# RetNet recurrence and a SiLU layer in split float32: remainders by VectorE alone, a fourth buffer for g, chunk 2's y read back at other places

## The chip, the cores and the metric

The kernel runs on one core of a Trainium2 chip. A core has TensorE (matrix products, into the accumulators of PSUM), VectorE, ScalarE and GpSimd (elementwise work), and SyncE, which here only issues DMAs. Each engine works through a queue of its own in order, and waits on semaphores for the others. The profile calls them PE (with PEld for its loads of weights), DVE, ACT, POOL and SP. The metric is the device time of one execution in microseconds; lower is better. The executions shown for the kernel before took 593.3, 593.84 and 3425.35 us, the last far out of line, and their median is 593.84.

## The reference

Two blocks follow each other: a recurrence over time for each head, and two dense layers with SiLU between them.

```python
# q, k, v: (4, 8, 768, 64) float32; w_in: (512, 2048), w_out: (2048, 512) float64
gamma = 1.0 - 2.0 ** (-5.0 - np.arange(H))
scale = 1.0 / np.sqrt(D)
for t in range(S):
    state = gamma[None, :, None, None] * state + einsum('bhd,bhe->bhde', k[:, :, t], v[:, :, t])
    y[:, :, t] = scale * einsum('bhd,bhde->bhe', q[:, :, t], state)
x = y.transpose(0, 2, 1, 3).reshape(B * S, H * D)      # 3072 x 512
h = x @ w_in
g = h * (1.0 / (1.0 + np.exp(-h)))
out = (g @ w_out).astype(np.float32)                   # 3072 x 512
```

## The kernel before, in words

**Chunks and units.** Time is cut into six chunks of 128 steps; with four batches that makes 24 units, numbered unit = 4 * chunk + batch. For a unit the kernel turns q and k (on TensorE for the early units, by a transposing DMA for the later ones), forms scores, masks them with the decay, carries a state, and forms y in PSUM. A "visit" of number m does the y of unit m - 2, the scores of unit m - 1 and, early on, the turning of unit m (`halves`, `visit`).

**Products in three parts.** TensorE multiplies in a reduced float32. Each operand is therefore split in three: a high part, a remainder, and a mixed part, and a product is the sum of three products (parts 0 and 1 into one accumulator, `ha` or `oa`, part 2 into another, `hb` or `ob`; an elementwise combination of the two gives the result). Slices of w_in and w_out are split by `split_steps`, x by `split_x` (ScalarE the high part, L653; VectorE the other two, L656 and L659), g by `split`. The weights arrive as 64-bit floats and are first converted with integer operations by `convert_steps` (L211 to L230).

**First layer.** A step (c, f) multiplies chunk c's x (512 tokens) by column block f of w_in: eight products into ha, four into hb (`multiply`, L754). `close_steps` then has ScalarE copy ha into a buffer of g (L777) and VectorE take hb from it (L782), and `put_g` stores g to DRAM (L796). Buffers of g are three tiles of tag `hs` in the pool `hpool`; ha and hb take turns in three banks of PSUM, so a bank has to be emptied before the second next accumulator can start.

**The order of the steps** is a list written out by hand: for chunks 0, 1 and 2 the blocks are woven together, and blocks 12 to 15 of chunks 0 and 1 and blocks 8 to 15 of chunk 2 come late: (0,12) to (0,15), (1,12) to (1,15), (2,8) to (2,15); then chunks 3, 4 and 5. `takes` names the steps after which a slice of weights is converted, `behind` the steps after which a visit or a `late_y` or `late_x` stands. A visit stands behind (1,15), one behind each of (2,9), (2,11) and (2,13).

**Chunk 2's x.** Its split form first lies in a tile of the pool `wpool` (tag `wq`), which is later needed for w_in's blocks 12 to 15. So y of chunk 2 is stored to DRAM, read back by `late_y` (L682) and split a second time by `late_x`, into the tile of `xpool` that chunk 0's x has left. Step (2,8) is the first that uses this second split. `late_y` takes its buffers by turns from tag `kt` and from tag `wl`, the tile that otherwise holds the unscaled remainder of a slice of weights.

**Second layer.** Chunk by chunk, `split` reads g back, applies SiLU and splits it; TensorE multiplies by w_out (L1270, L1294), and the results are stored.

**Queues.** TensorE's order is by hand throughout. That of the other engines is by hand for about the first 55 us; after that a scheduler places their instructions as the kernel is built, within the limits that `issue_after` sets. All DMAs are issued from SP's queue, in order: a DMA that waits there for a buffer or for data holds up all behind it. A tile of a pool waits for the last use of the tile whose buffer it takes. GpSimd does the `token` writes (a fence between products of one y, L412) and the copies ahead of a transposing DMA (L444).

The functions that the change touches, and what calls them, with the line numbers of the profile:

Of the kernel before, what the change touches and what calls it, by code (L numbers as in the profile page):

```python
# [12 lines left out]

FP32 = mybir.dt.float32
FP32R = mybir.dt.float32r
# [3 lines left out]
AF = mybir.ActivationFunctionType  # L19
# [15 lines left out]
def kernel(  # L35
# [52 lines left out]
    const = pool("const", 1)  # L88
    ld = pool("ld", 2)
    one = pool("one", 1)  # L90
    hpool = pool("hpool", 3)
    stage = pool("stage", 2)
    conv = pool("conv", 1)
    ps_u = pool("ps_u", 1, space=PS)
# [17 lines left out]
            quads[name] = wpool.tile([128, 4, 3, 512], FP32R, tag="wq", name=f"{name}4")  # L112
        return quads[name][:, f - NF + 4]

    def split_steps(f, w32, name, factor, to, behind_x=False):

        to[f] = w = w_slot(f, name)
        lo = conv.tile([128, 512], FP32, tag="wl", name=f"{name}l_{f}")
        yield
        with queue((held or evac or [None])[0] if behind_x or f >= NF - 4 else evac[0]):  # L120
            nc.scalar.activation(out=w[:, 0, :], in_=w32, func=AF.Copy, scale=HALF * factor)
        high = w[:, 0, :].bitcast(FP32)
        yield
        nc.vector.scalar_tensor_tensor(out=lo, in0=w32, scalar=factor, in1=high,  # L124
                                       op0=ALU.mult, op1=ALU.subtract)
        yield
        nc.scalar.activation(out=w[:, 1, :], in_=lo, func=AF.Copy, scale=1.0 / EPS)
        yield
        nc.vector.scalar_tensor_tensor(out=w[:, 2, :], in0=high, scalar=EPS, in1=lo,
                                       op0=ALU.mult, op1=ALU.subtract)  # L130

    def split_w(*of):
        steps = split_steps(*of)
# [20 lines left out]
    def load(name, n):  # L154
        if n >= len(units):
            return
        c, b = units[n]
        src = {"k": k, "q": q, "v": v}[name]
        if n == 4 * B and name == "k":
            t = conv.tile([128, H, D], FP32, tag="wl", name=f"kf_{n}")  # L160
            nc.sync.dma_start(out=t, in_=src[b, :, ds(c * C, C)].rearrange("h t d -> t h d"))
            kqv[name][n] = t
            return
        if n < EARLY:

            if n not in early:
                early[n] = wpool.tile([128, 3, H, D], FP32, tag=f"w{4 + n}", name=f"kqv_{n}")
            t = early[n][:, "kqv".index(name)]
        else:
            t = ld.tile([128, H, D], FP32, tag=f"{name}f", name=f"{name}f_{n}",  # L170
                        bufs=2 if name == "q" else 3)
        nc.sync.dma_start(out=t, in_=src[b, :, ds(c * C, C)].rearrange("h t d -> t h d"))
        kqv[name][n] = t
# [76 lines left out]
    def early_slice(i):  # L250

        out = []
        yield from convert_steps(i, out)
        yield
        steps = split_steps(i, out[0], "wi", scale, w_sb, None)
        next(steps)
        yield from steps

# [9 lines left out]
    def take_w(after=None, parts=False):  # L268

        i = taken[0]  # L270
        taken[0] += 1
        if i >= 2 * NF:
            return
        with queue(after) if after else ExitStack():
            rounded = convert_w(i)

        def finish():
            w32 = rounded()
            if i < NF:
                list(split_w(i, w32, "wi", scale, w_sb))  # L280
# [21 lines left out]
    def begin_w():  # L302

        i = taken[0]
        taken[0] += 1
        split = split_w(i, convert_w(i)(), "wi", scale, w_sb, True)
        next(split)
        half_split.append(split)

# [367 lines left out]
    y_late = {}  # L677

    def late_y(b):
        p, tag, bufs = ((one, "kt", 2), (conv, "wl", 1))[b % 2]  # L680
        y_late[b] = p.tile([128, KIN, C], FP32, tag=tag, name=f"yr_{b}", bufs=bufs)
        nc.sync.dma_start(out=y_late[b], in_=y_dram[b])  # L682

# [90 lines left out]

    def close_steps(c, f, ha, hb):
        hs = new_g(c, f)
        copied[:] = [nc.scalar.activation(out=hs, in_=ha, func=AF.Copy, scale=ONE_E).ins]  # L777
# [4 lines left out]
        taken_out[:] = [nc.vector.tensor_tensor(out=hs, in0=hs, in1=hb, op=ALU.subtract).ins]  # L782
        with queue(taken_out[0]):
            while behind_next:
                behind_next.pop(0)()
# [33 lines left out]
            w_got[f] = t  # L819

    def w_out(f, parts=False):
        steps = split_steps(f, w_got.pop(f), "wo", 1.0, wo)
# [330 lines left out]
    takes = [(1, 5)] + [(0, f) for f in range(6, half)]  # L1153
    takes += [(2, half - 4), (2, half - 2)]
    takes += [(0, half), (0, half + 3), (1, half + 1), (1, half + 3)]
    takes += [(0, NF - 3), (0, NF - 1), (1, NF - 3)]
    takes += [(3, f) for f in (0, 3, 7, 11, 14)]
    takes += [(4, f) for f in (0, 3, 7, 11, 14)]
    takes += [(5, f) for f in (2, 5, 8)]
# [6 lines left out]
    for i, x in enumerate(at):  # L1166
        behind[x] = lambda m=EARLY + 6 + i: visit(m)
    behind[0, NF - 2] = lambda: [late_y(b) for b in range(2)]
    behind[1, NF - 4] = lambda: [late_x(0), late_y(2), late_x(1), late_y(3)]
    behind[1, NF - 2] = lambda: [late_x(2), late_x(3)]  # L1170
    behind[1, NF - 1] = lambda: visit(EARLY + 6)


# [181 lines left out]
```

## Time and profile before

| what | value |
|---|---|
| median of the executions shown | 593.84 us |
| the profiled execution | 592.68 us, its span 590.9 us |
| TensorE busy | 579.3 us (98%) |
| VectorE busy | 401.1 us (68%), 672 instructions |
| ScalarE busy | 342.7 us (58%), 607 instructions |
| GpSimd busy | 34.1 us (6%) |
| DMA | 108.91 MB in 144336 packets, 184 GB/s on average |
| products of the first layer (L754) | ends near 337 us |
| granted TensorE clock | 0.998 on average |

The profile is of one execution. A row of a group gives the line, the engine, the operation and its tiles, how often it ran, the busy time in us and the mean of one in ns, and then how long the engine had been idle ahead of it and what ended that. A row of a timeline gives start and duration in us. In windows each engine has its busy time and its count, then come the granted clock, the share of the DMA engines, and GB/s. A busy TensorE is not a TensorE at its peak: the ends of products are modelled and they overlap, so their beat is read from starts.

### The profile page before, as it was taken

The page shows a single profiled execution, that of the slowest core. Times are in us where ns is not written, and L with a number is a line of the kernel's source. Part 1 is how long each engine was busy: PE and PEld are TensorE (multiplying, and loading weights), DVE is VectorE, ACT ScalarE, POOL GpSimd, SP SyncE. Part 2 cuts the span into 40 slices and gives each one's busy share as a digit, 9 for nine tenths or more (in the row PEclk, how much of TensorE's full clock was granted, in tenths as well). Part 3 has the DMA queues.
Part 4 walks back from the last instruction along what each step waited for, and adds up shares of the span by engine and source line. Part 5 has one row for each costly group of instructions (what it writes and reads, how often), then busy time and mean ns, then how long its engine had stood idle before and what let it go on. Part 6 is the DMA issues. An engine that isn't in the chain of part 4 may idle for free. (4 is left out here: it accounts for less than half of the span.)

```text
span 590.9 us, 13700 instructions
## 1 busy us (share of the span) xinstructions
PE 579.3 (98%) x5509; PEld 498.2 (84%) x5509; DVE 401.1 (68%) x672; ACT 342.7 (58%) x607; POOL 34.1 (6%) x89
## 2 busy tenths in 40 slices
PE   8999999999999999999999999999999999999996
PEld 6787888888788888888888888888888888888885
DVE  3887999678896767767779794745645463645632
ACT  7787767576656446655477695544644544545311
POOL 3000120100022111120000000000000000000000
PEclk9999999999999999999999999999999999999999
DMA  9989877786699699999667863532524433443301
GB/s 193 214 198 207 191 194 266 251 251 215 202 263 222 174 269 245 285 258 253 236 207 276 265 214 107 175 111 91 194 73 138 147 108 106 158 127 102 113 1 72
DMA packets 144336, 108.91 MB, mean 184 GB/s; under 512 B 101136, under 2 KB 109584, under 8 KB 144272
## 3 DMA queue, kind: packets, MB, share of 16 engines
q1 hardware_dynamic: 144272, 108.03, 65.3%
q8 instruction: 43, 0.70, 0.5%
q14 instruction: 21, 0.17, 0.1%
HBM read 66.06 MB, written 36.70 MB: 174 GB/s over the span
## 5 line engine op out<-in xcount | busy, mean ns | idle before, releaser
L754 PE MATMUL ha<-xt,wi 128*128 128x512 f32 x736 | 176.6, 382 | 0.6 <-DVE g L782 0.4
L754 PEld LDWEIGHTS ha<-xt,wi 128*128 128x128 f32 x736 | 137.1, 189 | 22.6 <-DVE g L782 2.6
L1270 PE MATMUL o<-wo,gs 128*128 128x512 f32 x564 | 137.1, 379 | 0.0
L1270 PEld LDWEIGHTS o<-wo,gs 128*128 128x128 f32 x564 | 106.6, 189 | 15.1
L846 DVE TENSOR_TENSOR gs<-gr,gs 128x512 fp32r<-128x512 f32 x96 | 62.1, 685 | 83.1 <-ACT gs L844 83.1
L1270 PE MATMUL oa<-wo,gs 128*128 128x512 f32 x376 | 111.8, 379 | 0.0
L843 ACT ACTIVATE gr<-gr 128x512 f32<-128x512 f32 x96 | 59.6, 629 | 65.5 <-DMA gr<-gd 64.2
L754 PE MATMUL hb<-xt,wi 128*128 128x512 f32 x368 | 95.0, 380 | 1.8 <-DVE gk L782 0.9
L777 ACT ACTIVATE g<-ha 128x512 f32<-128x512 f32 x87 | 51.8, 596 | 64.1 <-PE ha L754 49.8
L782 DVE TENSOR_TENSOR g<-g,hb 128x512 f32<-128x512 f32 x87 | 59.5, 684 | 41.7 <-ACT g L777 34.6
L754 PEld LDWEIGHTS hb<-xt,wi 128*128 128x128 f32 x368 | 69.1, 189 | 13.5 <-DVE gk L782 1.7
L1270 PEld LDWEIGHTS oa<-wo,gs 128*128 128x128 f32 x376 | 71.1, 189 | 10.1
L844 ACT ACTIVATE gs<-gr 128x512 fp32r<-128x512 f32 x96 | 53.3, 621 | 38.2 <-PE ob L1270 29.9
L1270 PE MATMUL ob<-wo,gs 128*128 128x512 f32 x188 | 71.3, 379 | 0.0
L847 DVE SCALAR_TENSOR_TENSOR gs<-gs 128x512 fp32r<-128x512 f32 x96 | 61.9, 683 | 0.1
L1270 PEld LDWEIGHTS ob<-wo,gs 128*128 128x128 f32 x188 | 35.5, 189 | 5.0
L211 ACT ACTIVATE ca<-wf 128x512 f32<-128x512 f32 x32 | 26.5, 827 | 20.1 <-DVE cs L224 11.2
L542 DVE TENSOR_TENSOR am<-sc,decay 128x512 f32<-128x512 f32 x24 | 16.5, 686 | 10.2 <-PE sc L534 8.7
L224 DVE SCALAR_TENSOR_TENSOR cs<-ca,cs 128x512 uint32<-128x512 uint32 x32 | 22.1, 690 | 0.8
L659 DVE SCALAR_TENSOR_TENSOR xt<-xt 128x512 fp32r<-128x512 f32 x28 | 20.8, 755 | 0.6
L582 PE MATMUL y<-qt,mid 64*64 64x64 f32 x376 | 19.4, 220 | 1.0 <-issue 1.0
L1319 DVE TENSOR_TENSOR o<-o,o 128x512 f32<-128x512 f32 x10 | 6.7, 687 | 17.4 <-ACT o L1318 17.4
(136 smaller groups left out, 611.3 us busy)
## 6 DMA issues: line engine op xcount, KB each, us to landing
gr<-gd SPq DMA_DIRECT2D x96, 256.0 KB, 2.8
gd<-g SPq DMA_DIRECT2D x87, 256.0 KB, 3.9
wf<-in_moe_w_out_dram SPq DMA_DIRECT2D x16, 512.0 KB, 4.6
out_dram<-o SPq DMA_DIRECT2D x23, 256.0 KB, 2.5
wf<-in_moe_w_in_dram SPq DMA_DIRECT2D x16, 256.0 KB, 4.2
wf<-in_moe_w_in_dram SPq DMA_DIRECT2D x32, 128.0 KB, 4.1
kf<-in_k_dram SPq DMA_DIRECT2D x16, 256.0 KB, 4.9
qf<-in_q_dram SPq DMA_DIRECT2D x16, 256.0 KB, 4.5
```

The lines of the kernel that those rows point to most:

```text
L211: top = nc.scalar.activation(out=a.bitcast(FP32), in_=hi.bitcast(FP32), func=AF.Abs, scale=2.0 ** -3).ins
L224: nc.vector.scalar_tensor_tensor(out=s, in0=a, scalar=3, in1=s, op0=ALU.logical_shift_left, op1=ALU.bitwise_xor)
L582: i = nc.tensor.matmul(to[ts(e, D), o, a, :], lhsT=lhsT, rhs=rhs, start=key not in started, stop=True, skip_group_check=True).ins
L659: nc.vector.scalar_tensor_tensor(out=x[2], in0=x[1].bitcast(FP32), scalar=-1.0 / EPS, in1=x[0].bitcast(FP32), op0=ALU.mult, op1=ALU.add)
L754: nc.tensor.matmul(hb if i == 2 else ha, lhsT=w_sb[f][:, i, ts(kk, 128)], rhs=woven(xt[c][:, i, kk, :]), start=kk == 0 and i != 1, stop=kk ...
L777: copied[:] = [nc.scalar.activation(out=hs, in_=ha, func=AF.Copy, scale=ONE_E).ins]
L782: taken_out[:] = [nc.vector.tensor_tensor(out=hs, in0=hs, in1=hb, op=ALU.subtract).ins]
L843: nc.scalar.activation(out=g, in_=g, func=AF.Silu)
L844: nc.scalar.activation(out=t[:, 0, :], in_=g, func=AF.Copy, scale=HALF)
L846: nc.vector.tensor_tensor(out=t[:, 1, :], in0=g, in1=high, op=ALU.subtract)
L847: nc.vector.scalar_tensor_tensor(out=t[:, 2, :], in0=t[:, 1, :].bitcast(FP32), scalar=-1.0 / EPS, in1=high, op0=ALU.mult, op1=ALU.add)
L1270: nc.tensor.matmul(o, lhsT=g, rhs=woven(wo[f][:, i, :], (c, b) == (NC - 1, B - 1)), start=f == 0 and i != 1, stop=f == NF - 1 and i != 0 o ...
```

## The change

`split_steps` no longer uses a tile for the unscaled remainder. Before, VectorE wrote the remainder there, ScalarE scaled it into part 1, and VectorE formed part 2 from the high part and the remainder. Now VectorE writes part 1 directly, as (w - high) * (1 / EPS), and part 2 as (high - part 1) * EPS, both by a custom VectorE operation, TENSOR_TENSOR_REDUCE_SUB_MAX, whose output is the scaled difference of two inputs. The factor `scale` that used to be put into w_in is put into the combination of ha and hb instead (`close_steps`): ScalarE's copy has it in its factor, and VectorE's subtraction becomes a scalar_tensor_tensor that multiplies hb by -scale and adds.

The tile that is freed (tag `wl`) makes room for a fourth buffer of tag `hs`. The load of k of unit 16, which lay in `wl`, now takes one of these. `late_y` takes its four buffers from `kt`, `hs`, `kt` and `qt`; all four reads are called for behind (0,14) and (0,15), where the last two were called for behind (1,12). The splits of batches 2 and 3 are called for behind (1,13) instead of (1,14). Three conversions of w_out slices move from behind (0,13), (0,15) and (1,13) to behind (2,10), (2,12) and (2,15).

```diff
-    hpool = pool("hpool", 3)
+    hpool = pool("hpool", 4)
...
+    def difference(out, a, b, factor):
+        nc.vector._custom_dve(TENSOR_TENSOR_REDUCE_SUB_MAX, out=out, in0=a, in1=b, s1=factor)
+
-    def split_steps(f, w32, name, factor, to, behind_x=False):
+    def split_steps(f, w32, name, to, behind_x=False):
...
-        lo = conv.tile([128, 512], FP32, tag="wl", name=f"{name}l_{f}")
+        high, low = (w[:, i, :].bitcast(FP32) for i in range(2))
...
-            nc.scalar.activation(out=w[:, 0, :], in_=w32, func=AF.Copy, scale=HALF * factor)
-        high = w[:, 0, :].bitcast(FP32)
-        yield
-        nc.vector.scalar_tensor_tensor(out=lo, in0=w32, scalar=factor, in1=high,
-                                       op0=ALU.mult, op1=ALU.subtract)
-        yield
-        nc.scalar.activation(out=w[:, 1, :], in_=lo, func=AF.Copy, scale=1.0 / EPS)
-        yield
-        nc.vector.scalar_tensor_tensor(out=w[:, 2, :], in0=high, scalar=EPS, in1=lo,
-                                       op0=ALU.mult, op1=ALU.subtract)
+            nc.scalar.activation(out=w[:, 0, :], in_=w32, func=AF.Copy, scale=HALF)
+        yield
+        difference(w[:, 1, :], w32, high, 1.0 / EPS)
+        yield
+        difference(w[:, 2, :], high, low, EPS)
...
-            t = conv.tile([128, H, D], FP32, tag="wl", name=f"kf_{n}")
+            t = hpool.tile([128, H, D], FP32, tag="hs", name=f"kf_{n}")
...
     def late_y(b):
-        p, tag, bufs = ((one, "kt", 2), (conv, "wl", 1))[b % 2]
+        p, tag, bufs = ((one, "kt", 2), (hpool, "hs", 4), (one, "kt", 2), (one, "qt", 3))[b]
...
-        copied[:] = [nc.scalar.activation(out=hs, in_=ha, func=AF.Copy, scale=ONE_E).ins]
+        copied[:] = [nc.scalar.activation(out=hs, in_=ha, func=AF.Copy,
+                                         scale=scale * ONE_E).ins]
...
-        taken_out[:] = [nc.vector.tensor_tensor(out=hs, in0=hs, in1=hb, op=ALU.subtract).ins]
+        taken_out[:] = [nc.vector.scalar_tensor_tensor(
+            out=hs, in0=hb, scalar=-scale, in1=hs, op0=ALU.mult, op1=ALU.add).ins]
...
-    takes += [(0, NF - 3), (0, NF - 1), (1, NF - 3)]
+    takes += [(2, NF - 6), (2, NF - 4), (2, NF - 1)]
...
-    behind[1, NF - 4] = lambda: [late_x(0), late_y(2), late_x(1), late_y(3)]
-    behind[1, NF - 2] = lambda: [late_x(2), late_x(3)]
+    behind[0, NF - 1] = lambda: [late_y(b) for b in range(2, B)]
+    behind[1, NF - 4] = lambda: [late_x(b) for b in range(2)]
+    behind[1, NF - 3] = lambda: [late_x(b) for b in range(2, B)]
```

More of the change, by code (lines that the diff above doesn't have):

```diff
@@ L12 @@
 from concourse._compat import with_exitstack
+from concourse.dve_ops import TENSOR_TENSOR_REDUCE_SUB_MAX
 FP32 = mybir.dt.float32
@@ L254, in early_slice @@
         yield
-        steps = split_steps(i, out[0], "wi", scale, w_sb, None)
+        steps = split_steps(i, out[0], "wi", w_sb, None)
         next(steps)
@@ L279, in finish @@
             if i < NF:
-                list(split_w(i, w32, "wi", scale, w_sb))
+                list(split_w(i, w32, "wi", w_sb))
             else:
@@ L305, in begin_w @@
         taken[0] += 1
-        split = split_w(i, convert_w(i)(), "wi", scale, w_sb, True)
+        split = split_w(i, convert_w(i)(), "wi", w_sb, True)
         next(split)
@@ L821, in w_out @@
     def w_out(f, parts=False):
-        steps = split_steps(f, w_got.pop(f), "wo", 1.0, wo)
+        steps = split_steps(f, w_got.pop(f), "wo", wo)
         for _ in range(3):
```

## The prediction

> **What bounds the kernel now.** The page's first part comes first, then the chain that ended last.
>
> ```profile
> PE 579.3 (98%) x5509; PEld 498.2 (84%) x5509; DVE 401.1 (68%) x672; ACT 342.7 (58%) x607; POOL 34.1 (6%) x89
> PE 43%; DMA 1%; DVE 0%; ACT 0%; DVEq 0%; issue 0%; ACTq 0%
> ```
>
> TensorE is the bound: it is busy 98% of the span, and the chain of the last 43% is TensorE alone. Nothing that VectorE or ScalarE saves is worth anything by itself; only a wait of TensorE that goes or comes counts. So the next view is the timeline of TensorE, to see what an undisturbed step costs and where steps are late.
>
> ```profile
> 104.11 1.89 PE L754 MATMUL ha<-xt,wi 128*128 128x512 f32 x8
> 105.84 1.03 PE L754 MATMUL hb<-xt,wi 128*128 128x512 f32 x4
> 106.70 1.67 PE L754 MATMUL ha<-xt,wi 128*128 128x512 f32 x7
> ...
> 159.29 1.99 PE L754 MATMUL ha<-xt,wi 128*128 128x512 f32 x8 [0.38 <-DVE g L782]
> 161.12 1.03 PE L754 MATMUL hb<-xt,wi 128*128 128x512 f32 x4
> 162.28 1.99 PE L754 MATMUL ha<-xt,wi 128*128 128x512 f32 x8
> ...
> 169.64 1.10 PE L754 MATMUL hb<-xt,wi 128*128 128x512 f32 x4 [0.55 <-DVE xt L659]
> ```
>
> The first three rows are the undisturbed beat: eight products into ha take 1.73 us (105.84 - 104.11), four into hb 0.86, a step 2.59. Against it the other rows are late: 162.28 comes 1.16 after 161.12 instead of 0.86 (0.3 lost), 159.29 follows VectorE by about as much again (0.4), and 169.64 comes 2.55 after the ha that starts at 167.09 (shown below) instead of 1.73 (0.8). VectorE ends the two that are labelled: it turns g late, or splits chunk 2's y late. These 1.5 us are what the moved work can give back. The other wait that the change aims at is that for a buffer of g:
>
> ```profile
> ACT g L777 <- DMA gd<-g: 10.7, 6, 3.4
> ...
> 327.18 5.94 DMA gd<-g
> 333.20 0.61 ACT g L777
> 333.86 1.13 PE hb L754 x4
> ```
>
> The first row is of the waits, the others of the chain: a store of g takes 5.94 us to land, ScalarE gets its buffer at 333.20, and hb starts right behind it at 333.86. ScalarE waits 10.7 us like this in all, but it passes little on: TensorE's next free bank is mostly still ahead. I credit 0.8 us at the end of the first layer and near 257 us together, within bounds of 0 and 1.5. From 337 us on the chain is an unbroken row of products, which the change does not touch.
>
> **Part 1: remainders by VectorE alone.** Each of 32 slices lost one ScalarE pass (L127), and keeps two VectorE passes.
>
> ```profile
> L127 ACT ACTIVATE wi<-wil 128x512 fp32r<-128x512 f32 x16 | 10.1, 630 | 4.3 <-DVE wil L124 4.1
> L124 DVE SCALAR_TENSOR_TENSOR wil<-cs,wi 128x512 f32<-128x512 f32 x16 | 11.8, 739 | 3.9 <-ACT wi L121 3.8
> L129 DVE SCALAR_TENSOR_TENSOR wi<-wi,wil 128x512 fp32r<-128x512 f32 x16 | 11.0, 689 | 0.4
> L230 DVE CUSTOM_DVE_ANT_0 cw<-wf,cs 128x1024 uint16<-128x1024 uint16 x16 | 13.3, 829 | 3.8 <-DMA wod<-cw 3.5
> L782 DVE TENSOR_TENSOR g<-g,hb 128x512 f32<-128x512 f32 x87 | 59.5, 684 | 41.7 <-ACT g L777 34.6
> L1322 DVE SCALAR_TENSOR_TENSOR o<-oa,o 128x512 f32<-128x512 f32 x1 | 0.7, 692 | 0.3 <-ACT o_right L1306 0.3
> ```
>
> ScalarE is freed of 32 x 0.63 = 20 us, all beside TensorE: its own load is 58%, so nothing is credited except in the first 95 us, the first half of them ordered by hand, where short ScalarE steps stand in TensorE's way: 0.4 us, from 0 to three passes of early slices (3 x 0.63 = 1.9). The new VectorE operation is not in the trace. Below, it cannot cost less than the pass it replaces by much (689); above, the other custom operation takes 829 for 1024 short words, and two passes of 689 would be 1.38. I take 0.70, nearest the row with the same 512 words, two inputs and one output; 64 of them then change VectorE by under 1 us in 401, at no cost. The subtraction of hb becomes a scaled one that reads PSUM: 692 (L1322) for 684 (L782), 96 x 8 ns = 0.8 us of VectorE, hidden in its idle third.
>
> **Part 2: y of chunk 2.** y of batch 0 goes where it went; batch 1 takes a g buffer; batch 2 waits for the buffer of batch 0. Batch 3 takes a buffer of tag qt, of which there are three. In the order to which the changed program is built, the read of batch 3 stands on SP behind the store of g(1,15), the load of v, and the transposing DMA of q of unit 15, and it waits for the last product of y of unit 12, since q of unit 12 held that buffer. That product is the last thing TensorE does before step (2,8), and step (2,8) is the first that needs the split of batch 3. So the step now waits for a whole chain. The place in the trace, POOL, TensorE, and SP:
>
> ```profile
> 166.15 0.09 POOL L412 MEMSET token<- 1x1 f32 x1 [51.18 <-PE y L582]
> 166.43 1.08 POOL L444 COPY kp<-kf 128x1024 uint16<-128x1024 uint16 x1 [0.19 <-POOL token L412]
> 167.45 1.50 POOL L444 COPY qp<-qf 128x1024 uint16<-128x1024 uint16 x1
> ...
> 166.94 0.22 PE L582 MATMUL y<-qt,state 64*64 64x64 f32 x2
> 167.09 0.48 PE L754 MATMUL ha<-xt,wi 128*128 128x512 f32 x1
> ...
> 171.45 1.36 SPq L455 DMA_TRANSPOSE qw<-qp  x1
> 172.90 0.53 SPq L172 DMA_DIRECT2D qf<-in_q_dram  x1
> ...
> 176.62 1.12 POOL L444 COPY qp<-qf 128x1024 uint16<-128x1024 uint16 x1 [2.15 <-DMA qf<-in_q_dram]
> ...
> L682 SPq DMA_DIRECT2D yr<-yd x4: 319/320/429, 130.6 to 160.4; - x4
> L653 ACT ACTIVATE xt<-yr x4: 621/626/630, 156.0 to 165.3; 128x512 fp32r<-128x512 f32 x4
> DMA to landing us min/median/max: 2.6/3.9/4.4
> ```
>
> Let T = 167.16 be the end of y's last product (166.94 + 0.22); before, step (2,8) starts at once. After: the copy into qp ends at 167.45 + 1.50 = T+1.8, shortened to T+1.6 since VectorE no longer works on chunk 2 beside it (the same copy takes 1.12 at 176.62). SP issues the transposing DMA, 1.4 us, until T+3.0. Then the read: from issue to landing 2.6 to 4.4 in the tile's view (its last line); the load of q that stood behind such a transpose, issued at 172.90, released POOL at 176.62, 3.7 later. I take 3.7: T+6.7. ScalarE's pass of 0.63 and two handovers of about 0.05: T+7.4. **TensorE stands still for 7.4 us.** Nothing covers it: its queue is in order, and all that is behind it waits. The floor is a free SP: 0.32 of issue is in the landing time, so 2.6 + 0.63 = 3.3; the ceiling is a copy at 1.5, a landing at 4.4 and a SP held 1 us longer, 9.3. The 0.8 us that were lost at 169.64 go, for lower and third parts of batch 3 follow within 1.4 us, ahead of hb's 1.73.
>
> **Part 3: the clock after a standstill.** The windows at the span's end, the chain's last products, and two groups:
>
> ```profile
> 588.00:588.50 0.50, 0.00 (x0) 0.00 (x0) 0.00 (x0) 0.00 (x0) 0.00 (x0) 1.00 0.90 299
> 588.50:589.00 0.50, 0.00 (x0) 0.00 (x0) 0.00 (x0) 0.00 (x0) 0.00 (x0) 0.55 0.64 217
> 589.00:589.50 0.50, 0.00 (x0) 0.00 (x0) 0.00 (x0) 0.00 (x0) 0.00 (x0) 0.50 0.16 49
> ...
> 585.80 0.46 PE oa L1294 x4
> ...
> L323 PE MATMUL idle<-zero 128*128 128x512 bf16 x2 | 1.0, 610 | 0.0
> L323 PE MATMUL sc<-zero 128*128 128x512 bf16 x3 | 0.8, 379 | 0.0
> ```
>
> The granted clock (third number from the right) falls from 1.00 to 0.50 at about 588.5; TensorE's last product ended at 586.26, so some 2.3 us without work were enough there. A standstill of 7.4 us should do the same. How long the slow clock lasts after work resumes is seen only at the start, where the fills of the idle tile at 2 to 3 us take 610 against 379 for the same shape later: slow for at least 2 us of work. By the rows a slow stretch between 2 and twice that costs half its length, 1 to 2 us, with 0 below (if the clock holds) and 3.4 above. I take 1.9.
>
> The Trainium skill, "TensorE: Matmul & The Clock Gate", Part 1: The HAM clock gate, says that the clock halves after an idle window of about 3.4 us and returns after about 3.4 us of sustained work, in windows that run freely. By it 1.7 us would be lost, and up to 3.4 with an unlucky window; the trace agrees on the halving, and no run here shows the return.
>
> **Part 4: three w_out slices later.** They leave steps (0,13), (0,15) and (1,13), whose room they gave to the splits above, for (2,10), (2,12) and (2,15).
>
> ```profile
> L214 DVE TENSOR_SCALAR cs<-wf 128x512 uint32<-128x512 uint32 x32 | 17.5, 548 | 0.2 <-DMA wf<-in_moe_w_in_dram 0.2
> L220 DVE TENSOR_SCALAR ca<-ca 128x512 f32<-128x512 f32 x32 | 13.5, 421 | 0.3 <-ACT ca L211 0.3
> L224 DVE SCALAR_TENSOR_TENSOR cs<-ca,cs 128x512 uint32<-128x512 uint32 x32 | 22.1, 690 | 0.8
> 180.00:195.00 15.00, 15.00 (x307) 12.99 (x306) 10.16 (x18) 7.59 (x13) 2.51 (x4) 1.00 1.21 222
> ```
>
> A slice costs VectorE 0.55 + 0.42 + 0.69 + 0.83 = 2.5 us (the last from L230 above). Two of them in the 15 us of the last row bring VectorE from 10.2 to 15.2: full. A subtraction may come late by the next step's 2.59 us before TensorE feels it, so I take 0.2 us, from 0 to 2. Their loads and stores move on SP too: the load for the next slice now waits there for a conversion, with stores of g and transposes behind it, under the same slack.
>
> **The sum.** Standstill 7.4, slow clock 1.9, crowding 0.2: 9.5 lost. Won: 0.7 at 159 and 162, of which I keep 0.5 since batch 2 is still read late; 0.8 at 169; 0.8 of g's buffer; 0.4 early: 2.5. Net +7.0 us. The profiled execution took 592.68 us, of which 590.9 are span, so it would become 599.7; the median of the runs shown, 593.84, would become 600.8. I say 600, +1.1%.
>
> **Rivals.**
> 1. *The read is quick*: POOL and SP are ahead, it lands in 2.6 us, standstill 5, clock slow for 1: net +3.5, about 596.5. For it: the smallest landing; against it: the transposing DMA stands right ahead. Chance 0.18.
> 2. *Not slower*: ScalarE's freed passes shorten the first 95 us by the full 1.9, g's buffer gives 1.5 and the moved slices 1.5; this decides once the standstill is at its floor of 3.3 and too short to cost clock: 3.3 - 4.9 = -1.6, about 592. For it: TensorE has many small waits there; against it: three conditions at once. Chance 0.05.
> 3. *The new VectorE operation takes two passes*: 0.69 more each; in 62 to 100 us, where VectorE has no idle time, five slices push 10 x 0.69 = 6.9 us onto TensorE, above the forecast: 607. For it: 829 of the other custom operation; against it: that one streams 1024. Chance 0.06.
> 4. *Crowding shows*: the moved slices hold a subtraction beyond its slack, or SP is held longer: 2 to 4 more, 602 to 604. For it: 15.2 of 15 us. Chance 0.14.
> 5. *The clock does not fall* (against Part 3): 598. Chance 0.12. By the Trainium skill's rule above this case is out.
> The forecast with its own spread of 2.5 has 0.45. That the change does not do what it says is the forecast itself: three batches are read sooner and the fourth later.
>
> **Chances.** 2% is 11.9 us, about what a measurement of this kernel can tell from no change: slower than 605.7 takes rival 3 and the ends of rival 4 and the forecast, 0.10; faster than 582 nothing reaches, 0.01; within, 0.89. The range of 595 to 605 leaves out rivals 2 and 3 and the low half of rival 1.
>
> **What would show it.** In the profile after: a gap of TensorE of 6 to 9 us ahead of an ha group near 166 us, put down to the pass that splits yr, and that pass waiting for the read's landing; a window of clock 0.50 behind it; no waits of ScalarE for gd near 333; the group of differences at about 0.70 us; steps near 159 on the beat. A gap under 3 us, or differences above 0.9, would make it wrong.

## The result, and the profile after

The changed kernel takes 602.9 us (median; 602.4 to 605.2) where the kernel before, timed beside it, takes 593.9: a ratio of 1.0178, 95% interval 1.0158 to 1.0198. It is slower by 9 us, and the interval is well clear of 1. The profiled execution took 602.43 us, 600.6 of them span; before it was 592.68 and 590.9. So 9.7 us of span are to be found.

The page's first part, and the first line of its chain (shares of the span by engine):

```profile
PE 580.8 (97%) x5509; PEld 499.8 (83%) x5509; DVE 401.7 (67%) x672; ACT 324.6 (54%) x575; POOL 33.1 (6%) x89
PE 82%; DVE 6%; DMA 5%; SPq 3%; issue 1%; ACT 1%; POOL 0%; DVEq 0%; POOLq 0%
```

ScalarE lost its 18 us, VectorE is where it was, and TensorE is still the bound. But the chain, which before was almost all TensorE as far as it could be followed (some 44% of the span), now also runs over VectorE, transfers and SP: TensorE waits for something. The timeline of TensorE around step (2,8) (start, duration, engine, line and operation; in brackets the idle time before it and what ended that):

```profile
158.67 1.89 PE L755 MATMUL ha<-xt,wi 128*128 128x512 f32 x8
...
161.26 1.89 PE L755 MATMUL ha<-xt,wi 128*128 128x512 f32 x8
...
165.81 0.23 PE L583 MATMUL y<-qt,state 64*64 64x64 f32 x2
172.54 3.78 PE L755 MATMUL ha<-xt,wi 128*128 128x512 f32 x8 [6.50 <-ACT xt L654]
...
179.86 0.69 PE L583 MATMUL y<-am,vf 64*64 64x64 f32 x32
```

Near 159 us the steps are back on the beat (158.67 to 161.26 is 2.59). Then y of unit 12 ends at 165.81 + 0.23 = 166.04, and step (2,8) starts at 172.54, 6.5 us later. Its eight products into ha then take 3.78 us, where 1.99 was usual. The chain of waits through this gap (start, duration, what):

```profile
166.28 1.05 POOL qp L445
...
167.35 1.30 SPq L456
...
168.71 3.13 DMA yr<-yd
...
171.86 0.64 ACT xt L654
```

It is the chain of the prediction, link by link: POOL's copy into qp, SP's transposing DMA, the read of batch 3's y, ScalarE's pass. The windows of 2 us (busy time of PE, PEld, DVE, ACT and POOL, then the granted clock, third from the right):

```profile
168.00:170.00 2.00, 0.00 (x0) 0.00 (x0) 0.20 (x1) 0.00 (x0) 0.00 (x0) 0.92 0.93 162
170.00:172.00 2.00, 0.00 (x0) 0.00 (x0) 0.00 (x0) 0.14 (x1) 0.00 (x0) 0.50 0.42 129
...
174.00:176.00 2.00, 2.00 (x6) 1.64 (x5) 0.00 (x0) 0.00 (x0) 0.00 (x0) 0.50 0.00 0
176.00:178.00 2.00, 2.00 (x9) 1.67 (x9) 0.56 (x1) 1.64 (x2) 0.00 (x0) 0.87 0.00 0
```

The clock falls within the standstill and is half until about 176.5 us. From the start of step (2,8) to the next product of y pass 179.86 - 172.54 = 7.32 us.

The second place is 40 us later; timelines of TensorE, VectorE and ScalarE:

```profile
210.67 1.99 PE L755 MATMUL ha<-xt,wi 128*128 128x512 f32 x8 [1.33 <-DVE g L784]
...
216.73 1.13 PE L755 MATMUL hb<-xt,wi 128*128 128x512 f32 x4 [1.47 <-ACT g L778]
218.20 1.99 PE L755 MATMUL ha<-xt,wi 128*128 128x512 f32 x8 [0.34 <-DVE g L784]
...
208.55 1.47 DVE L231 CUSTOM_DVE_ANT_0 cw<-wf,cs 128x1024 uint16<-128x1024 uint16 x1 [3.38 <-DMA wod<-cw]
...
214.98 0.71 DVE L231 CUSTOM_DVE_ANT_0 cw<-wf,cs 128x1024 uint16<-128x1024 uint16 x1 [2.02 <-DMA wod<-cw]
...
214.26 0.87 ACT L212 ACTIVATE ca<-wf 128x512 f32<-128x512 f32 x1 [4.57 <-DMA wf<-in_moe_w_out_dram]
```

TensorE waits for VectorE and ScalarE, but neither is short of time: VectorE stands idle for 3.38 and 2.02 us because the tile `cw`, of which there is one, still holds the slice before, whose store has not landed; ScalarE stands idle for 4.57 us because the next slice's load has not. Both work in order, so the subtraction and the copy of g that TensorE needs stand behind. The groups of the parts that were costed, and ScalarE's waits for a buffer of g:

```profile
L118 DVE CUSTOM_DVE_ANT_0 wi<-cs,wi 128x512 fp32r<-128x512 f32 x16 | 11.8, 738 | 3.9 <-ACT wi L126 3.3
L118 DVE CUSTOM_DVE_ANT_0 wi<-wi 128x512 fp32r<-128x512 f32 x16 | 11.0, 690 | 0.4
...
L784 DVE SCALAR_TENSOR_TENSOR g<-hb,g 128x512 f32<-128x512 f32 x87 | 59.7, 687 | 41.0 <-ACT g L778 24.4 <-PE hb L755 14.6 <-issue 0.7
...
ACT g L778 <- DMA gd<-g: 2.5, 1, 2.5
```

The new operation costs 738 and 690 ns, what the old remainders cost in the same places (739 and 689); the scaled subtraction 687 for 684; the waits for stores of g fell from 10.7 us to 2.5.

To see where the 9.7 us arise, take one and the same product in each kernel's trace and subtract its start before from its start after. Executions already differ by up to 0.8 us at the product into ha that starts at 55.8 us, so that difference is taken off, and the table says nothing of what lies ahead of it. Every kernel of the experiments is in the table (us later than before; a place is named by its time in the kernel before, so that the waits of the changed kernel at 210 to 218 us lie between 187.1 and 215.3):

| kernel | 157.0 | 164.1 | 187.1 | 215.3 | 292.8 | 336.6 |
|---|---|---|---|---|---|---|
| changed | -0.2 | -1.2 | +6.5 | +10.2 | +10.1 | +9.5 |
| e1 batch 3 in a buffer of g | -0.2 | -1.3 | -2.1 | +1.6 | +1.3 | +0.7 |
| e2 slices back | -0.2 | +0.3 | +9.3 | +9.3 | +8.9 | +8.4 |
| e3 both | -0.2 | 0.0 | 0.0 | +1.0 | +0.6 | +0.1 |
| e4 26 fills | -0.2 | -1.3 | +5.5 | +10.9 | +10.6 | +10.0 |
| e5 part 1 alone | -0.2 | -0.4 | -0.2 | -0.2 | -0.1 | -0.6 |
| e6 old places, four buffers | -0.2 | -0.6 | -0.6 | -0.6 | -1.0 | -1.5 |
| e7 two result tiles | -1.1 | -2.2 | +6.3 | +9.4 | +13.4 | +13.0 |
| e8 spaced | -0.2 | +0.1 | -0.7 | +0.2 | +1.2 | +0.7 |
| e9 even | -0.2 | -1.3 | -2.1 | -2.1 | +1.8 | +2.5 |
| e10 even, one early | -0.2 | -1.3 | -2.1 | -1.3 | +3.3 | +2.8 |
| e11 even, shifted | -0.2 | -1.2 | -2.1 | -2.1 | +1.2 | +3.1 |
| e12 20 fills | -0.2 | -1.3 | +6.7 | +10.2 | +10.7 | +10.2 |

Its first row is the result: 1.2 us won by 164 us, 7.7 lost at step (2,8), which hold 0.8 won near 169 us, 3.7 lost by 215 us, 0.7 won behind it. From 336.6 us to the end next to nothing changes (0.1 us).

### The profile page after: what moved, and what is told of

The parts are those of the page before. It is cut to its first block, busy times and chain, and to the rows that moved or that the text cites. A ratio compares the mean times of both kernels' runs of the same rounds, so it can differ in the third digit from the quotient of the medians.

```text
span 600.6 us, 13665 instructions
## 1 busy us (share of the span) xinstructions
PE 580.8 (97%) x5509; PEld 499.8 (83%) x5509; DVE 401.7 (67%) x672; ACT 324.6 (54%) x575; POOL 33.1 (6%) x89
## 4 chain that ended last, share of the span: by engine, by line
PE 82%; DVE 6%; DMA 5%; SPq 3%; issue 1%; ACT 1%; POOL 0%; DVEq 0%; POOLq 0%
PE ha L755 23%; PE o L1274 20%; PE oa L1274 14%; PE hb L755 11%; PE ob L1274 7%; PE y L583 3%; SPq L173 2%; DMA wod<-cw 2%; PE sc L525 1%; PE sc L535 1%; DMA yr<-yd 1%; DVE xt L657 1%; DMA kqv<-in_q_dram 1%; DMA vf<-in_v_dram 1%; DVE cs L215 1%
## 5 line engine op out<-in xcount | busy, mean ns | idle before, releaser
L784 DVE SCALAR_TENSOR_TENSOR g<-hb,g 128x512 f32<-128x512 f32 x87 | 59.7, 687 | 41.0 <-ACT g L778 24.4
L1274 PEld LDWEIGHTS oa<-wo,gs 128*128 128x128 f32 x376 | 71.1, 189 | 10.1
L231 DVE CUSTOM_DVE_ANT_0 cw<-wf,cs 128x1024 uint16<-128x1024 uint16 x16 | 14.2, 887 | 7.9 <-DMA wod<-cw 7.6
L660 DVE SCALAR_TENSOR_TENSOR xt<-xt 128x512 fp32r<-128x512 f32 x28 | 19.0, 689 | 0.6
```

The costliest lines, as they stand in the source:

```text
L660: nc.vector.scalar_tensor_tensor(out=x[2], in0=x[1].bitcast(FP32), scalar=-1.0 / EPS, in1=x[0].bitcast(FP32), op0=ALU.mult, op1=ALU.add)
L784: taken_out[:] = [nc.vector.scalar_tensor_tensor(out=hs, in0=hb, scalar=-scale, in1=hs, op0=ALU.mult, op1=ALU.add).ins]
L1274: nc.tensor.matmul(o, lhsT=g, rhs=woven(wo[f][:, i, :], (c, b) == (NC - 1, B - 1)), start=f == 0 and i != 1, stop=f == NF - 1 and i != 0 o ...
```

## The experiments

The theory: the read of batch 3's y waits for the last product of y of unit 12 and makes the standstill; the standstill makes the slow clock; slices that follow each other faster than a store and a load land make the second group of waits. Ratios are to the kernel before, timed beside each; 0.001 is 0.6 us.

### e1: batch 3's y in a buffer of g

```diff
     def late_y(b):
-        p, tag, bufs = (..., (one, "kt", 2), (one, "qt", 3))[b]
+        p, tag, bufs = (..., (one, "kt", 2), (hpool, "hs", 4))[b]
```

> The changed kernel, but y of batch 3 is read back into a buffer of g (tag hs) instead of one of tag qt, so that its read no longer waits for the last product of y of unit 12 and is issued some 35 us ahead of step (2,8). Theory (the wait for that read makes the standstill, and the standstill makes the slow clock): the 6.5 us ahead of step (2,8) and the 1.95 us of slow clock behind it go, the crowding at 208 to 218 us stays: 602.9 - 8.4 = about 594.5 us, 0.1% above before. Rival A (the standstill comes from y of unit 12 and the visit ahead of it, not from that read): TensorE still waits at 166 to 172 us, 600 us or more. Rival B (ScalarE's freed passes and the earlier splits are worth much, and were only hidden): 592 or less.

Measured: 594.06 us, ratio 1.0024 (1.0005 to 1.0042), 9.1 us better than the changed kernel's 1.0178. TensorE's timeline and a window:

```profile
166.35 1.99 PE L755 MATMUL ha<-xt,wi 128*128 128x512 f32 x8
...
171.73 0.69 PE L583 MATMUL y<-am,vf 64*64 64x64 f32 x32
...
202.64 1.99 PE L755 MATMUL ha<-xt,wi 128*128 128x512 f32 x8 [1.33 <-DVE g L784]
...
170.00:172.00 2.00, 2.00 (x25) 1.51 (x27) 1.37 (x3) 1.87 (x3) 0.00 (x0) 1.00 0.45 101
```

Step (2,8) starts at once behind y of unit 12 and the clock stays at 1.00: standstill and slow clock go with the one buffer, and the stretch from the step to the next product of y takes 171.73 - 166.35 = 5.38 us instead of 7.32. The second group of waits stays at 3.7 us, so it is no after-effect of the standstill. One number of the expectation was off: batch 3's read was issued 14 us ahead of the step (at 152.67) and not 35, as it stands behind stores of g on SP. Rival B is refuted: with the standstill gone, what is left of the change is not faster than before.

### e2: the three slices back at their old steps

```diff
-    takes += [(2, NF - 6), (2, NF - 4), (2, NF - 1)]
+    takes += [(0, NF - 3), (0, NF - 1), (1, NF - 3)]
```

> The changed kernel with the three w_out slices back at steps (0,13), (0,15) and (1,13). The read of batch 3 still waits for y of unit 12, but it now stands ahead of some stores on SP. Theory (the waits of 1.4, 1.6 and 0.5 us at 210 to 218 us come from slices converted too densely at (2,15), (3,0) and (3,3)): they go, 3.5 us; most of the 1.1 us that was won ahead of 164 us is given back; standstill and slow clock stay at 6 to 8.5 us: about 600 us, a ratio to before of 1.010. Rival (the second group of waits is an after-effect of the standstill, as everything behind it is pressed together): it stays and 602.9 or more is measured, a ratio of 1.015 to 1.018.

Measured: 601.34 us, ratio 1.0161 (1.0144 to 1.0178). The total gained 1.0 us, not 2.9, but the table shows each part: from 187 to 215 us it loses nothing more (+9.3, +9.3), so the second group of waits is gone as the theory has it, and 1.5 us are given back by 164. What was not expected is a longer standstill. SP's queue, TensorE's timeline, and the chain's piece:

```profile
169.05 3.27 SPq L683 DMA_DIRECT2D yr<-yd  x1
...
175.77 3.78 PE L755 MATMUL ha<-xt,wi 128*128 128x512 f32 x8 [7.81 <-ACT xt L654]
...
169.05 6.01 DMA yr<-yd
```

Here the read no longer stands behind the transposing DMA, and it is begun 1.1 us after y's end (167.96) instead of 2.7. Yet it landed later: SP took 3.27 us to issue it, where the changed kernel took 0.56, and it landed 6.01 us after it was begun. So a better place on SP's queue alone does not shorten the wait; that it goes when the read need not wait for y of unit 12, e1 shows.

### e3: both edits

```diff
-        p, tag, bufs = (..., (one, "kt", 2), (one, "qt", 3))[b]
+        p, tag, bufs = (..., (one, "kt", 2), (hpool, "hs", 4))[b]
...
-    takes += [(2, NF - 6), (2, NF - 4), (2, NF - 1)]
+    takes += [(0, NF - 3), (0, NF - 1), (1, NF - 3)]
```

> Both edits at once: batch 3's y read into a buffer of g, and the three slices back at (0,13), (0,15) and (1,13). Theory: standstill, slow clock and the waits at 210 to 218 us are all gone, and the waits at 169 us and for the store of g at 333 us stay gone as in the changed kernel: 602.9 - 8.4 - 3.5 + 1 = about 592 us, 0.3% below before. Rival (the two losses are one, and taking the first away already takes the second): the same time as with batch 3's y in a buffer of g alone, within 0.5 us.

Measured: 592.53 us, ratio 0.9998 (0.9982 to 1.0015). The two losses are two: with the first gone, taking the second away still wins 1.5 us over e1. The 0.3% below the kernel before that the theory had did not come; new waits took it, two of them in the chain:

```profile
152.72 4.83 DMA gd<-g
...
183.80 4.64 DMA kw<-kp
```

With two of the four buffers lent to y, a store of g that takes 4.83 us holds ScalarE (0.9 us of TensorE), and a transposing DMA takes 4.64 (1.0 us). A third wait, 0.67 us at 167.56 for VectorE's turn at g, takes most of what the earlier splits win near 169 us.

### e4 and e12: filling the standstill

```diff
-    FILL_P = {(0, 0): 1, (1, 0): 2}
+    FILL_P = {(0, 0): 1, (1, 0): 2, (2, 8): 26}
```

> The changed kernel with 26 products of the zero tile into the idle bank put ahead of step (2,8) (26 x 0.216 = 5.6 us at full clock), work that the reference does not ask for: TensorE is kept busy while it would wait for batch 3's y. Theory: the wait is as long as before, as the read sets its end, but the clock does not fall: of the 8.45 us only the slow clock's 1.95 goes, 602.9 - 1.9 = 601.0 us. Rival A (the slow windows come from elsewhere, or cost nothing): 602.9. Rival B (the fills are in the way, as the wait is shorter than them): above 603.

Measured: 602.51 us, ratio 1.0173 (1.0158 to 1.0188). The chain, TensorE and a window:

```profile
167.21 2.51 SPq L456
...
173.43 1.99 PE L755 MATMUL ha<-xt,wi 128*128 128x512 f32 x8 [1.82 <-ACT xt L654]
...
178.81 0.69 PE L583 MATMUL y<-am,vf 64*64 64x64 f32 x32
...
174.00:176.00 2.00, 2.00 (x11) 1.76 (x10) 0.80 (x2) 0.54 (x2) 0.00 (x0) 1.00 0.00 0
```

The clock holds at 1.00, and the same stretch of products takes 178.81 - 173.43 = 5.38 us instead of 7.32, as in e1: the slow clock's price in the changed kernel's trace is 1.94 us. But the total does not show it, for the transposing DMA took 2.51 us instead of 1.30, and near 198 us TensorE paused 1.6 us, put down to nothing in the trace. Whether that is chance or due to the fills, the second kernel was to tell:

```diff
-    FILL_P = {(0, 0): 1, (1, 0): 2, (2, 8): 26}
+    FILL_P = {(0, 0): 1, (1, 0): 2, (2, 8): 20}
```

> The changed kernel with 20 instead of 26 products of the zero tile ahead of step (2,8) (20 x 0.22 = 4.4 us), work that the reference does not ask for. With 26 the clock held, but the read came 1.0 us later (the transposing DMA ahead of it took 2.51 us instead of 1.30) and TensorE paused 1.6 us near 198 us with no cause shown, so that the time stayed. Theory A (those two were the draw of one execution): clock at 1.00 throughout, the standstill 6.5 us as without fills, 1.5 to 2 us under the changed kernel, a ratio of 1.0145 to 1.0155. Theory B (the fills themselves hold up the transfers, or TensorE's instructions): the transposing DMA takes over 2 us again or the pause comes again, a ratio of 1.017 or more. Theory C (a rest of some 2 us behind the fills is enough for the clock to fall): windows of 0.50 behind the standstill, 1.0175 or more.

Measured: 601.20 us (600.1 to 602.2), ratio 1.0145 (1.0128 to 1.0162), 2.0 us better than the changed kernel, theory A's number. The profiled execution, the longest of them, shows another picture, in the chain, TensorE's timeline and the windows:

```profile
166.41 2.12 SPq L456
...
165.03 4.49 PE L324 MATMUL ha<-zero 128*128 128x512 bf16 x20
172.16 3.68 PE L755 MATMUL ha<-xt,wi 128*128 128x512 f32 x8 [2.65 <-ACT xt L654]
...
199.65 2.00 PE L755 MATMUL ha<-xt,wi 128*128 128x512 f32 x8 [0.74 <-DVE state L555]
...
172.00:174.00 2.00, 1.83 (x5) 1.47 (x6) 1.39 (x2) 0.11 (x1) 0.00 (x0) 0.57 0.00 0
174.00:176.00 2.00, 2.00 (x7) 1.61 (x6) 0.00 (x0) 0.12 (x1) 0.00 (x0) 0.58 0.00 0
```

In it the clock fell at the end of a rest of 2.65 us (0.57 on average, theory C), where e4's rest of 1.82 us had left it at 1.00; the last section shows that the length of the rest does not decide alone. The transposing DMA again took over 2 us (half of theory B). The pause near 198 us came back in a smaller form, as a wait of 0.74 us at 199.65, which the profile puts down to VectorE's L555; e4's pause ended at 198.83, just when L555 did there, but that TensorE waited for it is not shown. The price of the slow clock thus rests on the stretch of products in e1 and e4, and not on the times of e12. Of its four executions, the two of 602.17 and 600.88 us ran at a mean granted clock of 0.996, below the 0.998 to 1.000 of the kernel before, so the clock fell in them; those of 601.51 and 600.09 us ran at 0.998 and 1.000. So the 2.0 us mix executions with the fall and without it. Whether fills lengthen the transposing DMA stays open: 2.51 and 2.12 us with them and 1.30 without at this place, but the changed kernel also has such DMAs of 1.82 and 2.19 us, at 192.65 and 197.16.

### e5 and e6: part 1 alone, and with four buffers

e5 is the kernel before with the remainders by VectorE and the factor at g, three buffers and `wl` kept. e6 adds the fourth buffer and lends buffers of g to batches 1 and 3 (and to k of unit 16), with reads, splits and slices at their old steps. Against the changed kernel, e5:

```diff
-    hpool = pool("hpool", 4)
+    hpool = pool("hpool", 3)
...
-        p, tag, bufs = ((one, "kt", 2), (hpool, "hs", 4), (one, "kt", 2), (one, "qt", 3))[b]
+        p, tag, bufs = ((one, "kt", 2), (conv, "wl", 1))[b % 2]
...
-    takes += [(2, NF - 6), (2, NF - 4), (2, NF - 1)]
+    takes += [(0, NF - 3), (0, NF - 1), (1, NF - 3)]
...
+    behind[1, NF - 4] = lambda: [late_x(0), late_y(2), late_x(1), late_y(3)]
+    behind[1, NF - 2] = lambda: [late_x(2), late_x(3)]
```

> The kernel before with part 1 alone: remainders by VectorE, the factor moved to g; three buffers for g, y of chunk 2 and the w_out slices at their old places. Theory: ScalarE's freed 18 us lie beside TensorE and buy nothing, a difference costs 0.69 us as before: a ratio to before of 0.999 to 1.001 (0.6 us), with TensorE's waits at 159, 169 and 333 us where they were. Rival A (freed ScalarE passes count in the first 95 us or at g): at least 1.5 us faster, a ratio of 0.9975 or less. Rival B (the new operation is dearer where it waits): 1.003 or more.

Measured: 592.24 us, ratio 0.9999 (0.9986 to 1.0013). Part 1 is worth no time that the interval shows: 18 us of ScalarE, and at most 0.8 us either way. The waits did not all stay where they were, though. In e5's trace TensorE no longer waits near 333 us (the table falls by 0.5 between 292.8 and 336.6), while ScalarE, with three buffers, waits there for a store as long as before (3.50 us, 3.31 before):

```profile
332.25 0.60 ACT L778 ACTIVATE g<-ha 128x512 f32<-128x512 f32 x1 [3.50 <-DMA gd<-g]
```

e6 differs from e5 in keeping `hpool` at 4 and in

```diff
-        p, tag, bufs = ((one, "kt", 2), (conv, "wl", 1))[b % 2]
+        p, tag, bufs = ((one, "kt", 2), (hpool, "hs", 4))[b % 2]
```

> The kernel before with part 1 and the fourth buffer for g: y of batches 1 and 3 is read into buffers of g at the old places, the slices are at the old places too. Theory: TensorE's wait behind the store of g near 333 us goes (0.5 us) and the one near 257 us (0.4), those at 159 and 169 us stay: a ratio to before of 0.998 to 1.000. Rival (two of the four buffers are lent to y from step (1,12) on, one fewer for g than before, and ScalarE waits for stores of g there): 1 us or more lost near 155 to 175 us, 1.002 or more.

Measured: 592.30 us, ratio 0.9996 (0.9982 to 1.0010), within the theory's range, and the rival's loss did not come (TensorE's wait for a split, in its timeline, is the one of before):

```profile
168.79 1.10 PE L755 MATMUL hb<-xt,wi 128*128 128x512 f32 x4 [0.54 <-DVE xt L660]
```

By the table the fourth buffer is worth 0.9 us in the profiled executions (-1.5 against -0.6), 0.4 of them by 187 us and 0.5 between 215 and 293 us; the timed interval does not tell that from nothing. Near 333 us e5 and e6 win the same 0.5, so it is not the fourth buffer that wins it.

### e7: two tiles for the converted slice

```diff
-    hpool = pool("hpool", 4)
+    hpool = pool("hpool", 3)
...
-        r = lo if i >= NF else conv.tile([128, DM], U32, tag="cw", name=f"cw_{i}")
+        r = lo if i >= NF else conv.tile([128, DM], U32, tag="cw", name=f"cw_{i}", bufs=2)
...
-        w = s if i < NF else conv.tile([128, DM], U32, tag="cw", name=f"cw_{i}")
+        w = s if i < NF else conv.tile([128, DM], U32, tag="cw", name=f"cw_{i}", bufs=2)
```

> The changed kernel, but with two tiles for the converted w_out slice instead of one and, for the room, three buffers for g instead of four; slices at the same steps, y of chunk 2 too. Theory A (the second group of waits, 3.6 us at 205 to 218 us, comes from the addition that waits until the last slice's store has left the one tile): TensorE's waits there fall to under 1 us, the standstill and the slow clock stay: 603 - 3 = about 600 us, a ratio of 1.012 to 1.014, if three buffers cost no more than the 0.5 to 0.8 us that the fourth has won. Rival (VectorE is simply full with two more slices, 15.2 us of work in 15, which the prediction priced): the waits stay and the ratio is 1.017 or more.

Measured: 602.57 us (601.2 to 605.8), ratio 1.0172 (1.0149 to 1.0196); the profiled execution is the longest of the four. VectorE's additions, and the chain:

```profile
206.97 0.83 DVE L231 CUSTOM_DVE_ANT_0 cw<-wf,cs 128x1024 uint16<-128x1024 uint16 x1
...
211.76 1.64 DVE L231 CUSTOM_DVE_ANT_0 cw<-wf,cs 128x1024 uint16<-128x1024 uint16 x1
...
203.32 5.38 DMA gd<-g
```

The additions no longer wait for the store (nothing in brackets), and TensorE's waits behind them are gone: from 210 us of this trace on it loses nothing for 40 us. But 3.1 us are lost between 187 and 203 us of the table's scale, most of it because a store of g took 5.38 us and ScalarE had no buffer, and 3.9 more near 258 us. There a store of g takes 6.35 us (261.46 in this trace) and a slice's load holds ScalarE for 4.15 us, both until about 267.7 us; TensorE waits 2.25 us, and the clock falls to half once more (0.50 in 270 to 272). With three buffers, one lent, stores of g are on the path. So theory A has the link right and the time wrong, for one shortage was exchanged for another. The rival's reason, VectorE full, doesn't hold in either kernel: it idled while TensorE waited in the changed one, and here it does the same work without those waits. One gain was not looked for: the tag `cw` also serves the slices of w_in, and e7 alone loses the two waits of 0.4 to 0.5 us for VectorE that every other trace has near 68 and 77 us, and its row stands at -1.1 at 157 us, where the others stand at -0.2. That the second tile does it is likely and not shown by itself: a second tile for the slice without a smaller `hpool` was not tried.

### e8 to e11: other steps for the slices

All four have batch 3's y in a buffer of g; only the steps of the slices differ.

```diff
-    takes += [(2, NF - 6), (2, NF - 4), (2, NF - 1)]
+    takes += [(0, NF - 3), (2, NF - 6), (2, NF - 3)]
```

> y of batch 3 in a buffer of g, as in the first of these kernels, and the three slices spaced: at (0,13), (2,10) and (2,13) instead of (2,10), (2,12) and (2,15). Theory: no standstill, and slices that are not pressed together against step (3,0) make TensorE wait for under 1 us at 200 to 220 us, while the beat at 159 us is kept: 0.5 to 1.5 us under before, a ratio of 0.9975 to 0.999. Rival (any slice that comes later is paid for in full): 1.001 or more.

Measured: 593.05 us, ratio 1.0008 (0.9997 to 1.0019), 0.2% short of the theory, whose range the interval leaves out, while the rival's 1.001 lies inside it. A store of g comes late near 159 us, as in e3, and a slice's load near 221 us; the chain's pieces:

```profile
153.41 4.90 DMA gd<-g
...
212.56 6.24 DMA wf<-in_moe_w_out_dram
```

The next three move the slices out of chunk 2. e9:

```diff
-    takes += [(2, NF - 6), (2, NF - 4), (2, NF - 1)]
-    takes += [(3, f) for f in (0, 3, 7, 11, 14)]
-    takes += [(4, f) for f in (0, 3, 7, 11, 14)]
-    takes += [(5, f) for f in (2, 5, 8)]
+    takes += [(3, f) for f in (0, 3, 6, 8, 11, 14)]
+    takes += [(4, f) for f in (0, 3, 6, 8, 11, 14)]
+    takes += [(5, f) for f in (2, 4, 6, 8)]
```

> y of batch 3 in a buffer of g, and no w_out slice in chunk 2 at all: the three slices are taken up by chunks 3 to 5, at steps 0, 3, 6, 8, 11 and 14 of chunks 3 and 4 and 2, 4, 6 and 8 of chunk 5 (every third step or so). Theory (the 3.6 us at 200 to 218 us are the price of two slices within less than the 6 us that a load and the 4 us that a store take, not of converting later): no wait there, the gains at 157 to 170 us (1.6), 258 (0.3) and 333 us (0.5) kept: 1.5 to 2.5 us under before, a ratio of 0.996 to 0.9975. Rival (later slices are always paid for, as VectorE and the transfers are full in chunks 3 to 5): waits of 1 us or more appear there, 0.999 or more.

e10 keeps (2, NF - 6) and (2, 5, 8) in chunk 5:

> As the kernel with even steps, but one of the three slices at (2,10), so that chunk 5 keeps its three. Theory: the slice at (2,10) has a step of 6.0 us without another slice on each side and costs nothing: the same 0.996 to 0.9975. Rival (its visits every second step leave no room for a load and a store in chunk 2): 1 to 2 us more than the kernel without it.

e11 has (2, 4, 7, 10, 12, 15) in chunks 3 and 4:

> As the kernel with even steps, but at steps 2, 4, 7, 10, 12 and 15 of chunks 3 and 4, so that each slice's load, which waits for the next turn of a unit, has other distances to its use (3 to 6 steps). Theory: as long as no two slices are within 5 us and a load has 3 steps (7.8 us) to land, the places do not matter: within 0.5 us of the kernel with even steps. Rival (a place beside a unit's visit costs): 1 us or more apart.

Measured: 595.98 us, ratio 1.0053 (1.0033 to 1.0074); 594.70, 1.0045 (1.0022 to 1.0069); 596.26, 1.0064 (1.0043 to 1.0085). The theory of e9 and e10 falls. e11, within 0.3 us of e9, came as it was expected, but with the loss of e9; e10 is neither as fast as its theory had it nor slower than e9, as its rival did. The stretch up to 215 us is clean, as it said (-2.1 in the table for e9 and e11, -1.3 for e10), but 4 to 5 us come back behind it. One of TensorE's waits in e9, and pieces of its chain:

```profile
257.17 1.13 PE L755 MATMUL hb<-xt,wi 128*128 128x512 f32 x4 [1.07 <-ACT g L778]
...
248.84 5.56 DMA wf<-in_moe_w_out_dram
...
315.46 4.79 DMA wod<-cw
```

It is the same two links as at 208 us, a load or a store of 5 us under an in-order ScalarE or VectorE, at other places. In e9, e10 and e11 the slices taken out of the steps of chunks 0 and 1 are paid for later. No kernel tried beats the one before beyond its interval; e6 comes nearest.

## Why the prediction was right, and where it was off

The time of 602.9 lies in the range, 2.9 us above the forecast of 600, and the main mechanism, a standstill behind batch 3's read with a slow clock after it, is the one that was forecast. By the forecast's own steps (us of the profiled executions):

- **Standstill: 7.4 said, 6.5 measured.** The links are those named, in their order, and e1 shows the cause. The copy ended at T+1.3 (1.6 said), the transposing DMA at T+2.6 (3.0), and the read landed at T+5.8 (6.7), after 3.13 us instead of 3.7.
- **Slow clock: 1.9 said, 1.94 measured**, from the same stretch with and without it (7.32 and 5.38). Rival 5 is out. That the number fits so well is in part luck. The length of the slow stretch was read off the fills at 2 to 3 us, where the windows of the kernel before show a granted clock of 1.00 (the trace has no record of the clock ahead of 4.87 us), so that row does not bear the reading out; and the price changes with the execution, as the last section shows.
- **What the moved work won: 0.5 near 159 and 162, 0.8 at 169 said; 1.0 and 0.8 measured.** The first is won by the slices that left: e2, which has them back, loses 0.5 there. The kernel before had more to give than was read off: its hb ahead of the step at 159.29 starts at 157.88, so by the beat that step comes 0.55 late and not 0.4.
- **Buffers of g: 0.8 said, 0.7 measured** (0.15 near 258 us, 0.55 near 333). The size is right and the reason for most of it is not: e5 wins the same 0.5 near 333 us with three buffers. What in part 1 wins it is not shown.
- **The first 95 us: 0.4 said, nothing measured** from 55.8 to 113 us (0.2 by 157). Ahead of 55.8 us the traces can't tell, as executions differ there by more; e5's time leaves room for 0.8 us at most.
- **New operation: 0.70 said, 0.68 to 0.74 measured**; rival 3 is out.
- **Crowding: 0.2 said, 3.7 measured.** This is the term that was mis-sized: rival 4 came true (602 to 604, given 0.14) beside the forecast. The step that failed is part 4's reasoning from VectorE's busy time, 15.2 us in 15, with a step of slack. In the trace VectorE is idle there. The bound of 2 us was for a late subtraction; what was late was a store and a load, which the part dismissed in one sentence ("Their loads and stores move on SP too"). The row that said so stood in the prediction: VectorE's addition into `cw` idled 3.8 us in all, 3.5 of them for the slice's store. After, the same group idles 7.9, 7.6 of them for the store:

```profile
L231 DVE CUSTOM_DVE_ANT_0 cw<-wf,cs 128x1024 uint16<-128x1024 uint16 x16 | 14.2, 887 | 7.9 <-DMA wod<-cw 7.6
```

The errors add up: 3.5 more for crowding, 0.8 less at step (2,8) (7.7 in the table, with the 0.8 won near 169 us, where 8.5 were said), 0.5 more won near 160, and 0.3 less won elsewhere, make 2.5 of the 2.7 us between 599.7 and 602.43. That the time stayed in the range is in part luck as well: two errors of 1.3 us together went against the 3.5 of the crowding.

## What to carry to other kernels

A buffer borrowed from another stage brings that stage's last reader along: before a tile's tag is changed, write down who must be done with it, what stands ahead of the new read on its queue, and how soon the first user comes; here one borrowed buffer cost 8.6 us more than another of the same size (+6.5 against -2.1 at 187.1 us, the changed kernel against e1), and that other one cost up to 0.9 us (e3). When work is moved, cost its transfers and its single tiles before its engine time: here a chain of store, addition, load and conversion through one tile set a pace of its own while the engines stood idle (e7 removes its first link, and the waits behind it go). An engine that is 58% busy and not on the path was worth nothing that could be measured when 18 us of it were freed (e5).

## What was not expected of the hardware

- Issuing a DMA is not of fixed cost: SP took 0.56 us for the read of y in the changed kernel and 3.27 for the same read in e2, and between 1.30 and 2.51 for the same transposing DMA (changed kernel, e4).
- The clock's changes lie a whole number of 3.4 us apart. Worked out from the windows' means, it was at half from 169.7 to 176.5 in the changed kernel (6.8 us), from 172.6 to 179.4 in e2 (6.8; means of 0.66 in 172 to 174 and 0.64 in 178 to 180), from 172.3 to 175.7 in e12 (3.4) and from 167.6 to 177.8 in e7 (10.2). The windows of e7 in which it fell and returned:

```profile
166.00:168.00 2.00, 0.00 (x0) 0.00 (x0) 1.55 (x3) 0.08 (x1) 0.68 (x1) 0.89 0.80 177
...
176.00:178.00 2.00, 2.00 (x6) 1.55 (x5) 0.78 (x2) 2.00 (x3) 0.00 (x0) 0.55 0.00 0
```

  So the fall has no fixed delay after the last product: 3.6 us in the changed kernel, 4.7 in e2, 2.8 in e12 (when products ran again since 172.16), 2.2 in e7, 2.3 at the end of the kernel before. The price is not fixed either: after the standstill, work went on at the slow clock for 4.0 us in the changed kernel, 3.4 in e12 and 6.2 in e7. The Trainium skill, "TensorE: Matmul & The Clock Gate", Part 1: The HAM clock gate, gives about 3.4 us for both and says that the windows run freely; the steps of 3.4 us agree. But a window need not be without work to bring the fall: in e7 products ran for the first 1.2 us of the last 3.4 us ahead of it, in the kernel before for 1.1.
- TensorE paused for 1.6 us within a group of products in e4, with no wait that the trace shows. No other trace has a pause within a group like it (e12's wait of 0.74 us near by stands between two groups), and its cause stays open.
